# Attention fused with two feed-forward stages: the newer scores' maximum ahead of the older exponents' second half on VectorE, and a second buffer for three blocks' halves

## The chip, the cores and the metric

The kernel runs on one core of one Trainium2 chip. The metric is the device time of one execution in microseconds (us); lower is better. Three runs of the kernel before gave 980.55, 981.07 and 977.10 us, a median of 980.55 us. One more execution was recorded by the hardware profiler, and every row below comes from that one.

## What is computed

Batch 4, 8 heads of 64, 576 positions, model width 512. All inputs and outputs are float32.

```python
# 1. attention, causal by blocks of 64 positions
scores = (q @ k.T) / 8, where a block of keys later than the query's block is masked
attn   = exp(scores - rowmax); attn = attn / (rowsum + 1e-9)
x      = concat_heads(attn @ v)                     # (4, 576, 512)
# 2. feed-forward 1, with a layer norm (weights 512x2048 and 2048x512)
x = x + relu(layernorm(x) * g_ln @ w1) @ w2
# 3. Fourier mixing, then feed-forward 2
u = x + real(fft(fft(x, axis=positions), axis=width))
out = u + relu(layernorm(u) @ v1) @ v2
```

## The kernel before, in words

**Precision by halves.** A float32 operand is split into two float16 halves, a high and a low one, and a product is three TensorE passes (high·high, high·low, low·high). ScalarE writes the high half as a copy, and VectorE then writes the low half as operand minus high half. This pair stands everywhere: for the exponents it is `P` (lines 941 and 942 in `p_split`), for a block's normalized rows `xs` (lines 594 and 616), for the hidden layer `hT` (lines 658 and 659).

**Blocks.** The 576 positions of each batch row are cut into 128-row pieces. Blocks `("E", b)` hold rows 0 to 255, blocks `("F", b)` most of the others, and block `"L"` the rows left over. Attention for the E blocks runs first. Attention for the later rows runs in 16 units (batch row × pair of heads) of three slots each: j = 2 and j = 3 are 128 query rows against 384 and 512 keys for two heads, and j = 4 is 64 rows of two heads against 576 keys. While these 16 units run, TensorE also works on feed-forward 1 of the blocks that are ready (E2, E3, F0, F1 in that stretch), and the two sorts of matmul are interleaved in TensorE's order.

**One slot of the later rows** is made of six steps that a table of lags (`LG`) spreads over following slots: `a_s` (scores on TensorE into the PSUM tile `st`, two buffers), `a_exp` (VectorE takes the row maximum, line 1196, and scales it, line 1197; ScalarE takes the exponent into `e`, line 1200, once for each head), `a_norm_p` (ScalarE's high half of `P`, line 941; VectorE's low half, line 942; then a DMA that transposes `P` into `PT`, line 948), `a_pv` (TensorE multiplies `PT` by the values into `pv`, line 913; `pv` has two PSUM buffers), and `a_evac` (VectorE takes `rr`, a reciprocal of the sums, lines 955 and 958, and writes the rows `N`, line 1245; for j = 4 ScalarE writes them, line 1251). In slot t, `a_exp` is that of the scores of slot t-1, and `a_norm_p` that of slot t-2. `RK` is the rank of each of the six in one slot's emission: before, `a_norm_p` (0) comes first, then `a_pv` (1), `a_evac` (2), `a_s` (3) and `a_exp` (4).

**What sets the order.** The program is emitted step by step by `merge`, and a scheduler with priorities (`prio`) makes of it one instruction list for each engine. Each engine works through its list in that order. `tc.issue_after(x)` keeps an instruction behind x. All DMAs with `SPq` in the rows stand in one issuing list (SP's).

**Layer norm of a block** (`ln`, `ln_hi`, `ln_lo`): for each of a block's two 128-row halves t, VectorE normalizes into `xn` (line 585), ScalarE copies to `xs` (594), VectorE subtracts (616), and a DMA transposes `xs` into `xnT` (617). `xs` has one buffer, so the copy for t = 1 waits until the transposing DMA for t = 0 has read it.

**Feed-forward 1:** `gemm1` (line 649) fills one of the `g` PSUM buffers with 24 matmuls; the pair 658/659 empties it. `gemm2` is line 675.

Of the kernel before, what the change touches and what calls it, by code (L numbers as in the profile page):

```python
# [9 lines left out]
F16 = mybir.dt.float16  # L10
# [3 lines left out]
AF = mybir.ActivationFunctionType  # L14
ALU = mybir.AluOpType
# [3 lines left out]
DM = H * D  # L19
# [7 lines left out]
G2P = 1  # L27
ST = 2
RVE = 1
LATE = ((1, ("F", 0)), (1, ("F", 1)))  # L30
RAWE = 3
AP = 20
# [11 lines left out]
NB = 1  # L44
# [5 lines left out]
PSC = 2.0 ** 14  # L50
# [33 lines left out]
EB = 3  # L84
RV = 2
PTB = 3
RK = (3, 4, 0, 1, 2, 5, 5.5)
PLAIN2 = (("E", 0), ("F", 0))
YP = 60
S7P = 400  # L90
# [10 lines left out]
def fused_kernel(ctx: ExitStack, tc: tile.TileContext, io: dict):  # L101
    nc = tc.nc
# [4 lines left out]
    fpool = ctx.enter_context(tc.tile_pool(name="fpool", bufs=1))  # L107
# [422 lines left out]
    def ln(ffn, c):  # L530
        with ExitStack() as order:
            if (ffn, c) in LATE:
                order.enter_context(tc.issue_after(ff_last["g"]))
# [44 lines left out]
    def ln_hi(ffn, c, t):  # L578
        mv, y = lnst[ffn, c]
        own = (ffn, c) in TURN  # L580
        if own:
            xn = a_tile([128, DM], F32, "xn0", "xn0")
        else:
            xn = fpool.tile([128, DM], F32, tag="xn", bufs=1, name="xn")
        done = nc.vector.tensor_scalar(
            out=xn, in0=X[c][:, t, :], scalar1=mv[:, t, 0:1], scalar2=y[:, t:t + 1],
            op0=ALU.subtract, op1=ALU.mult,
        )
        if (ffn, c, t) == (1, ("E", 0), 1):
            ff_last["n"] = done.ins  # L590
        if own:
            return ln_turn(ffn, c, t, xn)
        xs = fpool.tile([128, 2, DM], F16, tag="xs", bufs=1, name="xs")
        nc.scalar.activation(out=xs[:, 0, :], in_=xn, func=AF.Copy)
        lnst[ffn, c, t] = (xn, xs)

    def ln_turn(ffn, c, t, xn):

        ps = g_tile([128, 4, 128], "xt")
        with ExitStack() as order:  # L600
            if "f" in ff_last:
                order.enter_context(tc.issue_after(ff_last["f"]))
            for k in range(KT):
                nc.tensor.transpose(
                    out=ps[:, k], in_=xn[:, 128 * k:128 * k + 128], identity=A["unit"]
                )
        to = xnT[ffn, c][:, :, :, t * 128:(t + 1) * 128]
        nc.scalar.activation(out=to[:, 0], in_=ps, func=AF.Copy)
        nc.vector.tensor_tensor(out=to[:, 1], in0=ps, in1=to[:, 0], op=ALU.subtract)
# [12 lines left out]
    def ln_steps(ffn, c):  # L622
        return [
            (0.0, lambda: ln(ffn, c)), (0.0, lambda: ln_hi(ffn, c, 0)),
            (0.0, lambda: (ln_lo(ffn, c, 0), ln_hi(ffn, c, 1))), (0.0, lambda: ln_lo(ffn, c, 1)),
        ]
# [201 lines left out]
    A = {}  # L828
# [10 lines left out]
    def a_open(bufs):  # L839
        ap_["ctx"] = ExitStack()  # L840
        ap_["p"] = ap_["ctx"].enter_context(tc.tile_pool(name="apool", bufs=1))
        ap_["b"] = bufs

    def a_tile(shape, dt, tag, name):
        return ap_["p"].tile(shape, dt, tag=tag, bufs=ap_["b"][tag], name=name)

    def a_close():
        ap_["ctx"].close()
# [90 lines left out]
    def p_split(e, P, n):  # L939

        nc.scalar.activation(out=P[:, 0, 0:n], in_=e, func=AF.Copy, scale=PSC)  # L941
        nc.vector.scalar_tensor_tensor(  # L942
            out=P[:, 1, 0:n], in0=e, scalar=PSC, in1=P[:, 0, 0:n], op0=ALU.mult, op1=ALU.subtract
        )

    def p_turn(P, blocks):
        PT = a_tile([128, blocks, 128], F16, "PT", "PT")
        nc.sync.dma_start_transpose(out=PT, in_=P.rearrange("p a k -> p (a k)"))
        return PT
# [180 lines left out]
    def a_zeros():  # L1130


        A["qz"] = [a_tile([128, 640], F32, "qz", f"qz{i}") for i in range(QZ)]
        for z in A["qz"]:
            for h in range(2):
                nc.gpsimd.memset(z[HALF[1 - h], 256 + 64 * h:320 + 64 * h], 0.0)
# [54 lines left out]
    def a_exp(u, j):  # L1191
        st = A.pop(("st", u, j))
        nh, w = st.shape[1:]
        q = sm.tile([128, 2, 2], F32, tag="aq", bufs=4, name="aq")
        mx, nb = q[:, 0, 0:nh], q[:, 1, 0:nh]
        nc.vector.tensor_reduce(out=mx, in_=st, axis=AX.X, op=ALU.max)
        nc.vector.tensor_scalar(out=nb, in0=mx, scalar1=-0.125, scalar2=None, op0=ALU.mult)  # L1197
        e = a_tile([128, nh, w], F32, "e", "e")
        for h in range(nh):
            nc.scalar.activation(  # L1200
                out=e[:, h], in_=st[:, h], func=AF.Exp, scale=0.125, bias=nb[:, h:h + 1],
            )
        A["e", u, j] = e.rearrange("p h k -> p (h k)")

    def a_norm_p(u, j):
        e = A.pop(("e", u, j))
        n = e.shape[-1]
        full = -(-n // 128) * 128
        P = a_tile([128, 2, full], F16, "P", "P")
        if full > n:  # L1210
            nc.gpsimd.memset(P[:, :, n:full], 0.0)
        p_split(e, P, n)
        A["PT", u, j] = p_turn(P, 2 * full // 128)

    @prio
# [58 lines left out]
    def attention_items(order):  # L1274
# [3 lines left out]
        def at(t, rank, fn, *a):  # L1278
            ev.setdefault(t, []).append((rank, len(ev.get(t, [])), fn, a))
# [9 lines left out]
        for t, (u, j) in enumerate(units):  # L1289
            at(t, RK[0], a_s, u, j)  # L1290
            at(t + lag[1], RK[1], a_exp, u, j)
            at(t + lag[2], RK[2], a_norm_p, u, j)
            at(t + lag[3], RK[3], a_pv, u, j)
            at(t + lag[4], RK[4], a_evac, u, j)
            if j == 4 and u[1] == NPAIR - 1:
                at(t + lag[5], RK[5], a_x, u[0])
                gives[t + lag[5]] = ("X1", ("F", u[0]))
# [283 lines left out]
    if True:  # L1581
# [15 lines left out]
        def a_switch():  # L1597
            a_close()
            ap_["first"] = False
            a_open(dict(  # L1600
                rawv=RV, qz=QZ, k=KB, vh=VB, vl=VB,
                e=EB, P=2, PT=PTB, N2=NB, N3=NB, N4=NB,
            ))
            a_zeros()

# [7 lines left out]
        ap_["first"] = True  # L1613
        a_open(dict(stage=ST, rv=RVE, rz=RAWE, warm=1, vh=2, vl=2, e=E1B[0], P=E1B[1], PT=E1B[2], xnT0=1, xn0=X0B, unit=1))
        warm = a_tile([128, 1], F32, "warm", "warm")
# [6 lines left out]
        w_signs(ap_["p"], WN[0], NZ[0])  # L1622
        AE = [e_items(b) for b in range(B)]
        A1 = [(0.0, a_switch, (("W", 1, 2, 3), ("X1", ("E", 3))), None)]
        A1 += attention_items([(b, p) for b in range(B) for p in range(NPAIR)])
        A1 += [(0.0, a_end, (), ("X1", "L"))]
# [204 lines left out]
```

## Time and profile before

| | |
|---|---|
| median of three runs | 980.55 us |
| the profiled execution's own time | 978.52 us |
| its span, first to last instruction | 976.7 us |
| TensorE (PE) matmul busy | 926.3 us, 95% |
| VectorE (DVE) busy | 689.4 us, 71% |
| ScalarE (ACT) busy | 490.6 us, 50% |
| GpSimd (POOL) busy | 73.0 us, 7% |

The span is 1.82 us shorter than the time of the same execution; the rest lies outside the first and last instruction. TensorE is the busiest engine over the whole span, but the share is a mean over stages. The later rows' attention, which the change touches, lies between about 150 and 420 us from the start; what follows until 460 us is its last blocks' layer norm and feed-forward 1. In rows of the timeline, the bracket at a row's end is the idle time of that engine just before the row, and the instruction that ended it.

### The profile page before, as it was taken

To read this page: it belongs to the slowest core of one execution; us is meant where nothing else is said; L and a number is where in the kernel's file an instruction comes from. 1 tells how busy PE (TensorE), PEld (TensorE's weight loads), DVE (VectorE), ACT (ScalarE), POOL (GpSimd) and SP (SyncE) were. 2 spreads that over 40 slices of the span, in tenths; PEclk is the share of its full clock that TensorE was granted. 3 is DMA by queue.
4 is the path that set the end of the run, shared out by engine and by line. 5 is a ranking of instruction groups with operands and counts; after the bars stand their busy time and mean duration, and the time that the engine had idled before them with its cause. 6 is when DMAs were issued, how large, how long until landed. Compare 5 with 4: busy or idle time off the path is not lost.

```text
span 976.7 us, 19426 instructions
## 1 busy us (share of the span) xinstructions
PE 926.3 (95%) x7694; PEld 687.5 (70%) x7694; DVE 689.4 (71%) x1770; ACT 490.6 (50%) x860; POOL 73.0 (7%) x183
## 2 busy tenths in 40 slices
PE   8887789999998999999899999999999999999998
PEld 5766634664664664767476777757688888888887
DVE  4887877565667567576489998589486676665754
ACT  5787844555555554437556663335144252352431
POOL 1000000002011020050011211100000000000000
PEclk9799989999999999999999999999999999999999
DMA  8658636669668666568407775101110210101100
GB/s 281 201 178 224 150 71 174 133 126 167 134 135 157 130 141 97 97 167 310 108 6 218 261 252 184 27 11 65 33 23 23 44 23 23 33 23 34 23 23 22
DMA packets 159179, 110.68 MB, mean 113 GB/s; under 512 B 134182, under 2 KB 141351, under 8 KB 157041
## 3 DMA queue, kind: packets, MB, share of 16 engines
q1 hardware_dynamic: 154640, 104.87, 41.5%
q0 software_dynamic: 2336, 4.06, 1.6%
q8 instruction: 60, 0.98, 0.4%
q10 hardware_dynamic: 2112, 0.52, 0.2%
q14 instruction: 31, 0.25, 0.1%
HBM read 63.93 MB, written 11.01 MB: 77 GB/s over the span
## 4 chain that ended last, share of the span: by engine, by line
PE 43%; DVE 8%; DMA 3%; ACT 3%; issue 1%; POOL 1%; SPq 0%; ACTq 0%; POOLq 0%; DVEq 0%
PE g L721 15%; PE s L771 13%; PE g L649 5%; PE g L702 4%; PE g L675 3%; DMA wr<-in_w 2%; DVE wq L346 1%; DVE ws L225 1%; DVE hT L659 1%; ACT junk L246 1%; PE pq L1522 1%; PE ya L1492 1%; DMA xnT2('F', 0)_8056<-xs 1%; ACT sign L224 1%; DVE x L1442 0%
## 5 line engine op out<-in xcount | busy, mean ns | idle before, releaser
L649 PEld LDWEIGHTS <-wq 128*128 128x128 f16 x2112 | 203.5, 98 | 41.7 <-issue 14.7
L675 PE MATMUL g<-wq,hT 128*128 128x512 f16 x768 | 185.8, 386 | 2.6 <-ACT hT L658 2.2
L721 PEld LDWEIGHTS <-wq 128*128 128x128 f16 x1344 | 131.5, 98 | 15.4
L675 PEld LDWEIGHTS <-hT 128*128 128x128 f16 x768 | 75.1, 99 | 91.6 <-issue 7.5
L771 PEld LDWEIGHTS <-hs 128*128 128x128 f16 x1176 | 115.1, 98 | 13.3
L913 PE MATMUL pv<-vh,PT 128*128 128x65 f16 (+1 forms) x704 | 101.5, 201 | 20.3 <-DMA PT<-P 11.3
L738 ACT ACTIVATE hr<-g,tk 128x256 f32<-128x256 f32 x112 | 47.0, 471 | 143.7 <-PE g L721 143.7
L913 PEld LDWEIGHTS <-PT 128*128 128x128 f16 x1056 | 80.5, 100 | 35.0 <-issue 17.4
L942 DVE SCALAR_TENSOR_TENSOR P<-e,P 128x768 f16<-128x768 f32 (+2 forms) x56 | 54.7, 976 | 68.9 <-ACT P L941 68.8
L746 DVE TENSOR_TENSOR hr<-hr 128x128 f32<-128x128 f32 x224 | 65.5, 293 | 48.2 <-ACT hr L738 40.3
L1200 ACT ACTIVATE e<-st,aq 128x384 f32<-128x384 f32 (+2 forms) x80 | 49.1, 652 | 94.1 <-DVE aq L1197 91.6
L771 PE MATMUL s<-tT,hs 128*128 128x256 f16 x672 | 75.6, 273 | 0.0
L659 DVE SCALAR_TENSOR_TENSOR hT<-g,hT 128x512 f16<-128x512 f32 x88 | 59.7, 681 | 16.1 <-ACT hT L658 15.8
L702 PE MATMUL g<-wq,hT 128*128 128x512 f16 x288 | 66.6, 391 | 0.0
L658 ACT ACTIVATE hT<-g 128x512 f16<-128x512 f32 x88 | 51.6, 587 | 28.9 <-PE g L649 28.7
L913 PE MATMUL pv<-vl,PT 128*128 128x64 f16 (+1 forms) x352 | 61.9, 201 | 0.0
L753 DVE TENSOR_TENSOR hs<-hr,hs 128x896 f16<-128x896 f32 x56 | 60.7, 1085 | 0.5
L771 PE MATMUL s<-tB,hs 128*128 128x256 f16 x504 | 57.3, 273 | 0.0
L224 ACT ACTIVATE sign<-wr 128x512 f16<-128x512 bf16 (+1 forms) x48 | 46.5, 969 | 16.4 <-DMA wr<-in_w 13.0
L752 ACT ACTIVATE hs<-hr 128x896 f16<-128x896 f32 x56 | 53.1, 948 | 1.6 <-DVE hr L746 1.6
L702 PEld LDWEIGHTS <-hT 128*128 128x128 f16 x288 | 28.6, 101 | 33.6 <-issue 3.1
L225 DVE SCALAR_TENSOR_TENSOR ws<-wr,sign 128x512 int32<-128x512 int32 (+1 forms) x48 | 41.2, 864 | 13.9 <-ACT sign L224 13.4
(414 smaller groups left out, 1511.9 us busy)
## 6 DMA issues: line engine op xcount, KB each, us to landing
wr<-in_w SPq DMA_DIRECT2D x16, 1023.5 KB, 6.0
wr<-in_w SPq DMA_DIRECT2D x32, 511.8 KB, 5.2
rawv<-in_vt SPq DMA_DIRECT2D x16, 320.0 KB, 3.0
k<-in_kt SPq DMA_DIRECT2D x16, 288.0 KB, 3.6
d<-ws SPq DMA_DIRECT2D x4, 1024.0 KB, 4.8
ws<-d SPq DMA_DIRECT2D x4, 1024.0 KB, 5.4
wt<-d SPq DMA_DIRECT2D x4, 1024.0 KB, 4.8
qz<-in_qt SPq DMA_DIRECT2D x32, 80.0 KB, 3.2
```

The lines of the kernel that those rows point to most:

```text
L224: nc.scalar.activation(out=z[:, :, :, 1], in_=r.bitcast(BF16)[:, :, :, 2], func=AF.Copy)
L649: nc.tensor.matmul(out=ps[:, i, :], lhsT=w1(ffn, k, wh, m), rhs=xt[:, xh, k, :], start=(n == 0), stop=(n == 3 * KT - 1),)
L659: done = nc.vector.scalar_tensor_tensor(out=h[:, :, 1, :], in0=ps, scalar=0.0, in1=h[:, :, 0, :], op0=ALU.max, op1=ALU.subtract,)
L675: nc.tensor.matmul(out=ps, lhsT=h[f // 4][:, f % 4, hh, t * 128:(t + 1) * 128], rhs=w2(ffn, f, wh), start=(f == 0 and hh == 0 and wh == 0) ...
L702: nc.tensor.matmul(out=g2["b"][t], lhsT=h[f // 4][:, f % 4, hh, t * 128:(t + 1) * 128], rhs=w2(ffn, f, wh), start=(f == 0 and hh == 0 and ...
L721: nc.tensor.matmul(out=ps[:, q, :], lhsT=w1(2, k, wh, i + 8 * q), rhs=xt[:, xh, k, :], start=(n == 0), stop=(n == 3 * KT - 1),)
L746: done = nc.vector.tensor_tensor(out=r[:, o], in0=r[:, a], in1=r[:, b], op=op)
L752: nc.scalar.activation(out=h[:, 0], in_=r[:, 1:8], func=AF.Copy)
L753: nc.vector.tensor_tensor(out=h[:, 1], in0=r[:, 1:8], in1=h[:, 0], op=ALU.subtract)
L771: nc.tensor.matmul(out=ps, lhsT=h[:, hh, hb], rhs=T[nm][:, wh, i], start=(i == 0 and hh == 0 and wh == 0), stop=(i == 7 and hh == 1),)
L913: nc.tensor.matmul(out=out[..., 0:w], lhsT=l, rhs=v[..., 0:w], start=(n == 0), stop=(n == len(mm) - 1))
L942: nc.vector.scalar_tensor_tensor(out=P[:, 1, 0:n], in0=e, scalar=PSC, in1=P[:, 0, 0:n], op0=ALU.mult, op1=ALU.subtract)
```

## The change

Three things are changed in the code. `a_exp` gets rank -1 and so comes first in a slot's emission. In `a_norm_p` the two instructions of `p_split` stand in the open, and the second one (VectorE's low half) is kept behind the newest scaled maximum, which `a_exp` leaves in `A["max"]`. And for the blocks E3, F0 and F1 of feed-forward 1 the second half's `xs` (t = 1) gets a buffer of its own, `xs1`.

```diff
+OWN = ((1, ("E", 3)), (1, ("F", 0)), (1, ("F", 1)))
...
-RK = (3, 4, 0, 1, 2, 5, 5.5)
+RK = (3, -1, 0, 1, 2, 5, 5.5)
...
-        xs = fpool.tile([128, 2, DM], F16, tag="xs", bufs=1, name="xs")
+        if (ffn, c) in OWN and t:
+            xs = a_tile([128, 2, DM], F16, "xs1", "xs1")
+        else:
+            xs = fpool.tile([128, 2, DM], F16, tag="xs", bufs=1, name="xs")
...
-        nc.vector.tensor_scalar(out=nb, in0=mx, scalar1=-0.125, scalar2=None, op0=ALU.mult)
+        got = nc.vector.tensor_scalar(
+            out=nb, in0=mx, scalar1=-0.125, scalar2=None, op0=ALU.mult
+        )
+        A["max"] = got.ins
...
-        p_split(e, P, n)
+        nc.scalar.activation(out=P[:, 0, 0:n], in_=e, func=AF.Copy, scale=PSC)
+        with tc.issue_after(A["max"]):
+            nc.vector.scalar_tensor_tensor(
+                out=P[:, 1, 0:n], in0=e, scalar=PSC, in1=P[:, 0, 0:n],
+                op0=ALU.mult, op1=ALU.subtract,
+            )
...
-                e=EB, P=2, PT=PTB, N2=NB, N3=NB, N4=NB,
+                e=EB, P=2, PT=PTB, N2=NB, N3=NB, N4=NB, xs1=1,
```

VectorE's list in a unit beside feed-forward 1's `gemm1` of block F0, before. `aq` is the maximum, `P` the low half of the exponents (1024, 576 and 768 wide for j = 3, 4 and 2), `hT` the emptying of a `g` buffer (the number tells which), `pw` the scale of a later unit's values:

```order
L942 SCALAR_TENSOR_TENSOR P<-e,P 128x1024
L659 SCALAR_TENSOR_TENSOR hT<-g_4236,hT 128x2x256
L955 TENSOR_SCALAR rr<-pv,pw 128x2
L1196 TENSOR_REDUCE aq<-st 128x1
L958 RECIPROCAL rr<-rr 128x2
L1197 TENSOR_SCALAR aq<-aq 128x1
L1245 TENSOR_TENSOR N_3851<-pv,rr 128x128
L955 TENSOR_SCALAR rr<-pv,pw 128x2
L942 SCALAR_TENSOR_TENSOR P<-e,P 128x576
...
L659 SCALAR_TENSOR_TENSOR hT<-g_4319,hT 128x2x256
L865 TENSOR_SCALAR pw<-pw 128x1
L1196 TENSOR_REDUCE aq<-st 128x2
```

The same stretch after:

```order
L1200 TENSOR_REDUCE aq<-st 128x1
L663 SCALAR_TENSOR_TENSOR hT<-g_4236,hT 128x2x256
L959 TENSOR_SCALAR rr<-pv,pw 128x2
L1201 TENSOR_SCALAR aq<-aq 128x1
L1221 SCALAR_TENSOR_TENSOR P<-e,P 128x1024
L962 RECIPROCAL rr<-rr 128x2
L1257 TENSOR_TENSOR N_3857<-pv,rr 128x128
L663 SCALAR_TENSOR_TENSOR hT<-g_4319,hT 128x2x256
L1200 TENSOR_REDUCE aq<-st 128x2
L959 TENSOR_SCALAR rr<-pv,pw 128x2
L1201 TENSOR_SCALAR aq<-aq 128x2
L1221 SCALAR_TENSOR_TENSOR P<-e,P 128x576
```

The maximum of j = 4 (`128x1`) has moved from behind the 1024-wide low half to ahead of it, and the maximum of the next unit's j = 2 from behind the 576-wide low half to ahead of it. `hT` of buffer 4319 has moved from behind the 576-wide low half to ahead of both that and the maximum. `N_3857` (the tile that was `N_3851`), which had no low half between it and the maximum of its slot, now has the 1024-wide one there.

VectorE's list in the layer norm of block F0, before (`xn` and `xs` as above; `N` is the rows of j = 2):

```order
L1161 SCALAR_TENSOR_TENSOR vl_3625<-rawv_3590,pw,vh_3624 128x10x64
...
L585 TENSOR_SCALAR xn<-XxF_2958,ln1('F', 0)_3924 128x512
L942 SCALAR_TENSOR_TENSOR P<-e,P 128x768
L616 TENSOR_TENSOR xs<-xn,xs 128x512
L585 TENSOR_SCALAR xn<-XxF_2958,ln1('F', 0)_3924 128x512
L1196 TENSOR_REDUCE aq<-st 128x2
L955 TENSOR_SCALAR rr<-pv,pw 128x2
L1197 TENSOR_SCALAR aq<-aq 128x2
L616 TENSOR_TENSOR xs<-xn,xs 128x512
L958 RECIPROCAL rr<-rr 128x2
L1245 TENSOR_TENSOR N_3773<-pv,rr 128x128
```

And after:

```order
L586 TENSOR_SCALAR xn<-XxF_2958,ln1('F', 0)_3924 128x512
L1165 SCALAR_TENSOR_TENSOR vl_3631<-rawv_3590,pw,vh_3630 128x10x64
L620 TENSOR_TENSOR xs<-xn,xs 128x512
L586 TENSOR_SCALAR xn<-XxF_2958,ln1('F', 0)_3924 128x512
L620 TENSOR_TENSOR xs_4025<-xn,xs_4025 128x512
L1200 TENSOR_REDUCE aq<-st 128x2
L959 TENSOR_SCALAR rr<-pv,pw 128x2
L1201 TENSOR_SCALAR aq<-aq 128x2
L1221 SCALAR_TENSOR_TENSOR P<-e,P 128x768
L962 RECIPROCAL rr<-rr 128x2
L1257 TENSOR_TENSOR N_3779<-pv,rr 128x128
```

The second `xs` now has a tile of its own (4025) and stands ahead of the maximum of j = 3; the 768-wide low half has moved from between the two `xn` to behind that maximum, just ahead of the reciprocal and `N`; and `vl`, the low half of a unit's values, which stood ahead of the first `xn`, stands behind it.

## Rows read from the trace of the kernel before

**Rows 1.** The page's head: the span.

```profile
span 976.7 us, 19426 instructions
```

**Rows 2.** Windows: busy of PE, PEld, DVE, ACT, POOL; TensorE clock; DMA share; GB/s.

```profile
150.00:460.00 310.00, 294.60 (x2557) 191.75 (x2556) 205.39 (x545) 163.67 (x285) 39.34 (x95) 0.99 0.68 149
```

**Rows 3.** Waits: who waited for whom; us in total, times, longest.

```profile
ACT e L1200 <- DVE aq L1197: 91.6, 45, 3.2
DVE P L942 <- ACT P L941: 68.8, 42, 2.3
```

**Rows 4.** Timeline of PE: start, us, what; in brackets idle before and releaser.

```profile
200.59 1.03 PE L649 MATMUL g<-xnT1('E', 2)_2013,wq 128*128 128x256 f16 x8 [2.06 <-DVE pw L865]
...
226.39 0.22 PE L913 MATMUL pv<-vh,PT 128*128 128x130 f16 x1 [2.22 <-DVE aq L1197]
...
271.76 1.58 PE L649 MATMUL g<-xnT1('E', 3)_2990,wq 128*128 128x256 f16 x13 [1.78 <-DVE hT L659]
...
309.56 0.27 PE L913 MATMUL pv<-vh,PT 128*128 128x130 f16 x1 [3.57 <-DVE N L1245]
...
349.02 1.03 PE L649 MATMUL g<-xnT1('F', 0)_3946,wq 128*128 128x256 f16 x8 [1.72 <-DVE pw L865]
...
378.72 0.19 PE L913 MATMUL pv<-vh,PT 128*128 128x65 f16 x1 [0.74 <-DVE N L1245]
```

**Rows 5.** Windows around two of these gaps; the last three columns are clock, DMA, GB/s.

```profile
224.00:228.00 4.00, 1.78 (x12) 0.90 (x12) 1.75 (x5) 2.14 (x4) 1.33 (x3) 0.94 0.58 116
228.00:232.00 4.00, 4.00 (x21) 2.07 (x20) 1.85 (x5) 2.24 (x3) 2.07 (x4) 0.63 1.04 231
308.00:312.00 4.00, 2.44 (x12) 1.45 (x13) 3.10 (x7) 2.50 (x4) 0.20 (x1) 0.68 0.67 117
312.00:316.00 4.00, 4.00 (x29) 2.01 (x28) 2.37 (x9) 2.71 (x6) 0.53 (x2) 0.89 0.98 212
```

**Rows 6.** Timeline of ACT and DVE in the layer norms of E3 and F0.

```profile
224.69 0.63 ACT L594 ACTIVATE xs<-xn 128x512 f16<-128x512 f32 x1 [3.16 <-DMA xnT1('E', 3)_2990<-xs]
...
301.72 0.55 DVE L585 TENSOR_SCALAR xn<-XxF,ln1('F', 0)_3924 128x512 f32<-128x512 f32 x1
...
307.66 0.63 ACT L594 ACTIVATE xs<-xn 128x512 f16<-128x512 f32 x1 [4.49 <-DMA xnT1('F', 0)_3946<-xs]
...
308.32 0.69 DVE L616 TENSOR_TENSOR xs<-xn,xs 128x512 f16<-128x512 f32 x1 [2.16 <-ACT xs L594]
...
309.12 0.29 DVE L1245 TENSOR_TENSOR N<-pv,rr 128x128 f32<-128x128 f32 x1
```

**Rows 7.** Timeline of ACT and DVE around the gap that ends at 349.02.

```profile
345.15 0.74 ACT L1200 ACTIVATE e<-st,aq 128x576 f32<-128x576 f32 x1 [2.44 <-DVE aq L1197]
...
346.64 0.76 DVE L942 SCALAR_TENSOR_TENSOR P<-e,P 128x576 f16<-128x576 f32 x1 [1.25 <-ACT P L941]
...
347.24 0.58 ACT L658 ACTIVATE hT<-g 128x512 f16<-128x512 f32 x1
...
348.28 0.68 DVE L659 SCALAR_TENSOR_TENSOR hT<-g,hT 128x512 f16<-128x512 f32 x1
...
349.98 0.88 DVE L1161 SCALAR_TENSOR_TENSOR vl<-rawv,pw,vh 128x640 f16<-128x640 f32 x1
```

**Rows 8.** Groups by line: shapes, count | busy us, mean ns | idle before, releasers.

```profile
L942 DVE SCALAR_TENSOR_TENSOR P<-e,P 128x768 f16<-128x768 f32 (+2 forms) x56 | 54.7, 976 | 68.9 <-ACT P L941 68.8
...
L1196 DVE TENSOR_REDUCE aq<-st 128x2 f32<-128x768 f32 (+2 forms) x48 | 46.6, 970 | 0.0
```

**Rows 9.** Timeline of SP, POOL and PEld from 240 to 245 us.

```profile
240.43 1.44 SPq L948 DMA_TRANSPOSE PT<-P  x1
...
242.12 0.78 PEld L913 LDWEIGHTS <-PT 128*128 128x128 f16 x18
...
244.28 0.20 POOL L1211 MEMSET P<- 128x128 f16 x1 [9.46 <-DMA PT<-P]
```

**Rows 10.** Timeline of PE behind the stage.

```profile
479.03 11.22 PE L675 MATMUL g<-wq,hT 128*128 128x512 f16 x42 [2.21 <-ACT hT L658]
```

## The prediction

> **What bounds the kernel now.** I read the views in this order: the windows, to see which stage has idle time on the busiest engine; TensorE's timeline in that stage, for the gaps and what ended them; the waits of VectorE and ScalarE; and the timelines of both just ahead of each gap.
>
> The profiled execution took 978.52 us, of which 976.7 is the span [rows 1]. The change touches the attention of the later rows, in the window from 150 to 460 us. There TensorE is busy for 294.60 of 310 us while VectorE is busy for 205.39 and ScalarE for 163.67 [rows 2]. So the stage runs at TensorE's pace with 310 - 294.6 = 15.4 us of gaps, and these are what an order of VectorE's list can win. Five gaps hold 2.06 + 2.22 + 1.78 + 3.57 + 1.72 = 11.35 us of it; each was ended by VectorE [rows 4]. The other 4.05 us lie in short gaps, like the one of 0.74 [rows 4].
>
> The five are of two sorts. At 226.39 and 309.56 a `pv` product waits for a PSUM buffer that the rows `N` empty. In both, ScalarE had been standing before the layer norm's second `xs`, 3.16 and 4.49 us, because the DMA that reads the first one had not landed; behind it VectorE stood 2.16 us at the low half of `xs`, with `N` behind that in its list [rows 6]. These two gaps also cost clock. In the 8 us around the first the granted clock was 0.94 and 0.63, around the second 0.68 and 0.89 [rows 5]: each time 4 x (0.06 + 0.37) or 4 x (0.32 + 0.11) = 1.72 us of full-speed work, part of it spent at the lower level, 1.2 GHz. At 200.59, 271.76 and 349.02 `gemm1` waits for a `g` buffer, that is for `hT`. In the last of them ScalarE's exponent had waited 2.44 us for VectorE's maximum, ScalarE's half of `hT` came only at 347.24 and VectorE's at 348.28, behind the low half of `P`, for which VectorE had itself waited 1.25 us [rows 7]. It is a ping-pong: over the run ScalarE's exponents wait 91.6 us for maxima, VectorE's low halves 68.8 us (42 times, 1.6 each) for ScalarE's high halves [rows 3]. Neither engine is full; each stands idle for the other.
>
> **The change part by part.** No arithmetic is added. VectorE issues as many maxima and low halves as before, of mean 0.97 and 0.98 us [rows 8]; only their places move.
>
> *Second buffer, block E3.* Its second `xs` can now be made together with the first, long before 224 us, so the 3.16 us wait goes. The gap of 2.22 us goes with it, and the 1.72 us of clock: 3.94 us.
>
> *Second buffer, block F0.* ScalarE's 4.49 us wait goes, but the new order puts other work ahead of `N`. From the start of the first `xn` the list now holds `xn` 0.55, `vl` 0.88, `xs` 0.69, `xn` 0.55, ScalarE's copy 0.63, `xs` 0.69, a maximum 0.97, the low half 0.98 and `N` 0.29 [rows 6 to 8]: 6.2 us, with three small ones about 6.7 (an estimate: 0.5 for the three). Before, it was 309.12 + 0.29 - 301.72 = 7.7. So `N` gains 1.0 us by its own list, and up to 1.6 more where the first `xn` itself starts earlier by one removed wait for a high half [rows 3]. Of the 3.57 us then 1.0 to 2.6 are left; I take 1.3, a saving of 2.3, since one slot's wait is likely gone. With so short a gap I take the 1.72 us of clock as saved too: 4.0 us. F1 has no gap of this sort among the five; its buffer counts as nothing.
>
> *Maximum first, beside `gemm1`.* Where the gap ended at 349.02, the maximum of j = 4 no longer stands behind a low half, so the exponent's 2.44 us go, and `hT` of the waiting buffer now precedes the next maximum and low half. `hT` comes at least 2.44 us earlier against a gap of 1.72 [rows 4, 7]. The gaps at 200.59 and 271.76 wait for the same thing. All three: 5.56 us. Next to be late there is `hT` behind `vl` in the same unit, whose place does not change.
>
> *The short gaps.* Of 4.05 us I take 1.0 as gone; zero and 4.05 are the ends.
>
> *TensorE's own list.* 48 more `pv` matmuls than before follow another `pv` matmul instead of a longer one. Eighteen in a row had their weights loaded in 0.78 us, 0.043 each [rows 9], so at most 48 x 0.043 = 2.1 us and at least nothing. Beside a longer matmul they were not free either; I take 0.7.
>
> *What is added as waits.* The low half of a slot now waits for the next slot's scores and maximum, and behind it in VectorE's list stand `rr`, `N` and `hT`. With slots of about 270 us / 48 = 5.6 us the scores are there a slot ahead in the units I followed, so the low half is not later than before by more than the maximum it lets pass. The transposing DMA behind it took 244.28 - 240.43 = 3.85 us until `P` was free again [rows 9], and its product comes two slots later, so it is covered. In SP's list the two query loads of most units now stand ahead of j = 3's transposing DMA. Their issue is not among my rows; the nearest is the 1.44 us of a transposing one, so 0 to 2.9 us late, under the same two slots. A wait of one more `N` here and there is likely; I take 2.0 us for new gaps in all, between 0 and the 15.7 us worked out under the third rival.
>
> *Sum.* 3.94 + 4.0 + 5.56 + 1.0 - 0.7 - 2.0 = 11.8 us, so 978.52 - 11.8 = 966.7 us against the profiled execution. Its 978.52 lies 2.03 below the median of the runs (980.55). I add half of that and predict 968 us. If every gap and both clock losses went, 15.4 + 3.4 = 18.8 us, it would be 960 us.
>
> **Rivals.**
>
> *Only the buffer pays.* The gaps before `gemm1` and before `pv` would then come from there being two `g` and two `pv` buffers, and an order of VectorE would move them, not remove them. For it: all five gaps wait for a PSUM buffer [rows 4]. Against it: the buffers' readers are late because VectorE and ScalarE stand idle, not because they are busy [rows 2, 3]. Gain 3.94 + 4.0 - 0.7 = 7.2, so 972 us. The Trainium skill, "Perfetto Trace Analysis", section Optimization Strategy, says that bubbles which repeat on the engine that ought to be full can mean too few PSUM or SBUF buffers. By that rule the three gaps of about 1.9 us, one in each stretch of `gemm1`, stay, and this rival is the outcome.
>
> *Given back later.* At 479.03 TensorE waits 2.21 us for ScalarE's `hT` [rows 10], in a stretch where ScalarE and VectorE prepare the second feed-forward's weights. If that preparation sets the pace and does not start earlier, TensorE only waits longer there: no change, 978 to 980 us. Against it: the preparation is started by the end of the attention, which moves with TensorE.
>
> *Slower: `N` behind the low half.* In every slot the low half, 0.98 us, now stands between the maximum and `N`. Each `N` frees one of two `pv` buffers, and the gap of 0.74 us ended by `N` [rows 4] shows that there is little spare time. If VectorE does not get its removed waits (1.6 us each) back ahead of `N`, each of the 16 units loses one 0.98: 15.7 us, of which the buffer's 7.2 are taken off, so 8.5 us slower, 988 us. It decides if `N` leaves later than before by more than the spare time once in a unit. The Trainium skill, "TensorE: Matmul & The Clock Gate", section on the architecture of the array, calls the lists of ScalarE and VectorE strict FIFO. The trace agrees, the `N` of 309.12 stood behind an `xs` it does not need [rows 6]; so one late high half would hold back everything.
>
> **How the numbers follow.** My forecast has a chance of 0.55 (962 to 971 us), only the buffer 0.18 (972), given back 0.17 (979), slower 0.10 (988). Half a percent of the median is 4.9 us, about what a measurement of this kernel can tell: faster means under 975.6, slower over 985.5. Faster: all of the forecast, 0.16 of the second and 0.04 of the third, 0.75. Slower: 0.08 of the last. The same: the other 0.17. The range is 960, where all gaps are gone, to 980, where nothing is gained; it leaves out little but the slower case.
>
> **What would show it.** Right: in the profile after, ScalarE's waits for maxima and VectorE's for high halves fall well under half of 91.6 and 68.8 us; TensorE's gaps between 150 and 460 us shrink from 15.4 to about 6; there is no wait of ScalarE at the second `xs` of E3 and F0, and the granted clock stays at 1.00 around E3's. Wrong: waits at `gemm1` for `hT` as long as before (then the buffer counts decide), new gaps before `pv` ended by `N` once in a unit (the slower case), or a longer gap than 2.21 us near 470 us (given back).

## The result, and where the profile after shows the time

The change took 966.3 us (median of four runs, 962.85 to 968.14) against 980.81 us of the kernel before (four runs, 977.1 to 983.43): a ratio of 0.9849, interval 0.9823 to 0.9875. Measured once more, among the experiments, it was 968.44 us and 0.9857 (0.9834 to 0.988). The profiled execution of the kernel after took 966.11 us, of which 964.3 is the span, 12.4 us less than [rows 1]. The forecast was 968 us.

In the kernel after, `gemm1` is line 653, `hT` 662 and 663, `pv` 917, the maximum 1200 and 1201, the exponent 1207, the halves of `P` 1219 and 1221, `xs` 598 and 620, `N` 1257 and 1263. First the page's head, and the window of the later rows' attention, with the columns of [rows 2]:

```profile
span 964.3 us, 19399 instructions
```

```profile
150.00:460.00 310.00, 305.46 (x2658) 200.84 (x2657) 215.87 (x574) 175.63 (x310) 42.14 (x96) 1.00 0.67 155
```

TensorE's gaps in it fell from 15.4 to 4.5 us, and the granted clock is at 1.00. The waits, as in [rows 3]:

```profile
ACT e L1207 <- DVE aq L1201: 64.1, 40, 5.0
...
DVE hT L663 <- ACT hT L662: 37.0, 36, 2.4
...
DVE vl L1165 <- ACT vh L1164: 16.8, 13, 1.8
...
ACT P L1219 <- DMA PT<-P: 15.5, 10, 3.0
```

VectorE's wait for the high half of `P`, 68.8 us before, is down to 1.8 us; ScalarE's wait for the maximum, 91.6 us before, fell by 30% only. Three waits are longer: VectorE's for `hT` (15.8 us before) and for `vh`, the high half of a unit's values (2.7 us before), and ScalarE's for the transposing DMA that frees a buffer of `P` (1.3 us before), because the low half, and with it that DMA, now comes later. TensorE's timeline, as in [rows 4] and [rows 10]:

```profile
301.29 0.22 PE L917 MATMUL pv<-vh,PT 128*128 128x130 f16 x1 [2.27 <-DVE N L1257]
...
367.31 0.19 PE L917 MATMUL pv<-vh,PT 128*128 128x65 f16 x1 [0.98 <-DVE N L1257]
...
410.98 9.22 PE L679 MATMUL g<-wq,hT 128*128 128x512 f16 x42 [0.36 <-DVE hT L663]
...
465.19 12.12 PE L679 MATMUL g<-wq,hT 128*128 128x512 f16 x54 [2.25 <-ACT hT L662]
...
545.39 0.39 PE L1534 MATMUL pq<-c_so,y 128*128 128x128 f16 x2 [2.07 <-ACT y L1511]
```

Of the five gaps of [rows 4] one is left, F0's, and that shortened; beside `gemm1` none is left. The row at 465.19 answers to [rows 10], and it comes 13.84 us earlier.

To size each term I take the start of one and the same matmul in both traces: the one that masks the scores of a unit's first slot (`MATMUL st<-never,late`). That of the fourth unit, before, after, and in the trace of the second measurement, whose profiled execution took 974.84 us:

```profile
195.61 0.20 PE L935 MATMUL st<-never,late 64*128 64x64 bf16 x2
```

```profile
197.71 0.20 PE L939 MATMUL st<-never,late 64*128 64x64 bf16 x2
```

```profile
200.97 0.20 PE L939 MATMUL st<-never,late 64*128 64x64 bf16 x2
```

| stretch, by the clock of before (us) | what lay there before | took before | took after | saved | took, second trace |
|---|---|---|---|---|---|
| 0 to 195.61 | ahead of the first gap | 195.61 | 197.71 | -2.10 | 200.97 |
| 195.61 to 213.65 | gap at 200.59 | 18.04 | 15.82 | 2.22 | 15.82 |
| 213.65 to 233.43 | gap at 226.39 (E3) and its clock | 19.78 | 15.73 | 4.05 | 15.73 |
| 262.68 to 280.45 | gap at 271.76 | 17.77 | 15.82 | 1.95 | 15.82 |
| 294.41 to 315.44 | gap at 309.56 (F0) and its clock | 21.03 | 18.14 | 2.89 | 19.86 |
| 344.38 to 362.08 | gap at 349.02 | 17.70 | 15.82 | 1.88 | 15.82 |
| 395.01 to 479.03, the row of [rows 10] | short gaps | 84.02 | 82.44 | 1.58 | 82.29 |
| the other four in between | short gaps | 105.08 | 103.71 | 1.37 | 106.24 |
| 479.03 to the end | | 497.67 | 499.11 | -1.44 | 500.55 |

The sum saved is 12.4 us. The stage itself, from the second row to the next to last, took 283.42 us before and 267.48 after and so saved 15.94 us; the rest was lost ahead of it and behind it. In the second trace the stage took 271.58 us and saved 11.84. What was saved at E3 and beside `gemm1` is the same there to 0.01 us. The 4.10 us between the two executions lie at F0 (1.72 us: about the same gap, but with a loss of clock behind it) and around F1 (2.52 us). In the second trace:

```profile
304.61 0.22 PE L917 MATMUL pv<-vh,PT 128*128 128x130 f16 x1 [2.34 <-DVE N L1257]
...
374.46 0.19 PE L917 MATMUL pv<-vh,PT 128*128 128x65 f16 x1 [2.26 <-DVE N L1257]
...
472.55 1.80 PE L679 MATMUL g<-wq,hT 128*128 128x512 f16 x4 [2.24 <-ACT hT L662]
```

F1's gap, the second row, was 0.98 us in the first trace.

### The profile page after: what moved, and what is told of

Read it like the earlier page. It is cut to its first block, busy times and chain, and to the rows that moved or that the text cites. A ratio compares the mean times of both kernels' runs of the same rounds, so it can differ in the third digit from the quotient of the medians.

```text
span 964.3 us, 19399 instructions
## 1 busy us (share of the span) xinstructions
PE 924.6 (96%) x7694; PEld 689.5 (72%) x7694; DVE 688.7 (71%) x1770; ACT 491.8 (51%) x860; POOL 74.8 (8%) x183
## 4 chain that ended last, share of the span: by engine, by line
PE 46%; DVE 7%; DMA 4%; ACT 3%; issue 1%; POOL 0%; SPq 0%; ACTq 0%; POOLq 0%
PE g L725 15%; PE s L775 13%; PE g L653 7%; PE g L679 4%; PE g L706 4%; DMA wr<-in_w 2%; DVE wq L347 1%; ACT junk L247 1%; DVE ws L226 1%; PE pq L1534 1%; DMA xnT2('F', 0)_8056<-xs 1%; ACT sign L225 1%; PE ya L1504 1%; DVE hT L663 1%; PE pv L917 1%
## 5 line engine op out<-in xcount | busy, mean ns | idle before, releaser
L679 PE MATMUL g<-wq,hT 128*128 128x512 f16 x768 | 180.5, 379 | 3.0 <-ACT hT L662 2.2
L725 PEld LDWEIGHTS <-wq 128*128 128x128 f16 x1344 | 131.5, 98 | 15.4
L917 PE MATMUL pv<-vh,PT 128*128 128x65 f16 (+1 forms) x704 | 98.4, 201 | 15.7 <-DMA PT<-P 10.7
L917 PEld LDWEIGHTS <-PT 128*128 128x128 f16 x1056 | 76.4, 99 | 34.0 <-DMA PT<-P 15.9
L1207 ACT ACTIVATE e<-st,aq 128x384 f32<-128x384 f32 (+2 forms) x80 | 48.9, 652 | 64.8 <-DVE aq L1201 64.1
L706 PE MATMUL g<-wq,hT 128*128 128x512 f16 x288 | 66.0, 388 | 0.0
L917 PE MATMUL pv<-vl,PT 128*128 128x64 f16 (+1 forms) x352 | 58.7, 200 | 0.0
L1200 DVE TENSOR_REDUCE aq<-st 128x2 f32<-128x768 f32 (+2 forms) x48 | 46.7, 973 | 12.5 <-PE st L939 9.4
L1219 ACT ACTIVATE P<-e 128x768 f16<-128x768 f32 (+2 forms) x48 | 41.2, 858 | 17.4 <-DMA PT<-P 15.5
```

The costliest lines, as they stand in the source:

```text
L679: nc.tensor.matmul(out=ps, lhsT=h[f // 4][:, f % 4, hh, t * 128:(t + 1) * 128], rhs=w2(ffn, f, wh), start=(f == 0 and hh == 0 and wh == 0) ...
L706: nc.tensor.matmul(out=g2["b"][t], lhsT=h[f // 4][:, f % 4, hh, t * 128:(t + 1) * 128], rhs=w2(ffn, f, wh), start=(f == 0 and hh == 0 and ...
L725: nc.tensor.matmul(out=ps[:, q, :], lhsT=w1(2, k, wh, i + 8 * q), rhs=xt[:, xh, k, :], start=(n == 0), stop=(n == 3 * KT - 1),)
L917: nc.tensor.matmul(out=out[..., 0:w], lhsT=l, rhs=v[..., 0:w], start=(n == 0), stop=(n == len(mm) - 1))
```

## The experiments

My theory after the result: the new order ends the gaps beside `gemm1`, the buffer those in the layer norms, and the two add up. The rivals: one part does it all, or the gaps beside `gemm1` end because of another place of `hT`, not because the ping-pong of ScalarE and VectorE ends. Each ratio below is to the kernel before on the same chip (medians 980.85 to 982.14 us); it is not quite the quotient of the two medians, from which it differs by up to 0.2%.

**The buffer alone.**

```diff
-RK = (3, -1, 0, 1, 2, 5, 5.5)
+RK = (3, 4, 0, 1, 2, 5, 5.5)
...
-        with tc.issue_after(A["max"]):
...
```

> Only the second xs buffer for E3, F0, F1; ranks and low half's place as before. Theory A (two parts that add: the buffer ends the gaps in the layer norms, the order those before gemm1): gap of 2.22 us at E3 gone with its clock loss, gap of 3.57 us at F0 down to 1 to 2 us, the three gemm1 gaps of about 1.9 us each still there; 6 to 9 us faster than before, ratio 0.991 to 0.994. Rival B (the order alone does it): ratio 0.999 to 1.001. Rival C (only the buffer pays, the order only moves gaps): ratio as the full change, 0.983 to 0.988.

Measured: 977.2 us, ratio 0.9951 (0.9933 to 0.997), less than theory A expected. **The order alone:**

```diff
-OWN = ((1, ("E", 3)), (1, ("F", 0)), (1, ("F", 1)))
+OWN = ()
```

> Ranks and the low half behind the newer maximum as in the change, xs with one buffer for all blocks. Theory A: the three gemm1 gaps gone (5.6 us) and most short gaps, the gaps at E3 and F0 still there at 2 to 4 us each with clock loss; 5 to 8 us faster, ratio 0.992 to 0.995. Rival B: ratio as the full change, 0.983 to 0.988. Rival C: ratio 0.999 to 1.001, gemm1 gaps of about 1.9 us still there.

Measured: 972.15 us, ratio 0.9913 (0.9886 to 0.994), more than theory A expected. The product of the two, 0.9864, is near the change's 0.9849: as far as the intervals tell, the parts add on time. Neither does it all. TensorE's timeline with the buffer alone, and then with the order alone:

```profile
201.50 1.03 PE L653 MATMUL g<-xnT1('E', 2)_2013,wq 128*128 128x256 f16 x8 [1.74 <-DVE pw L869]
...
225.36 0.22 PE L917 MATMUL pv<-vh,PT 128*128 128x130 f16 x1 [0.27 <-DVE N L1256]
...
306.67 0.22 PE L917 MATMUL pv<-vh,PT 128*128 128x130 f16 x1 [2.16 <-DVE N L1256]
```

```profile
234.78 0.20 PE L917 MATMUL pv<-vh,PT 128*128 128x65 f16 x1 [1.06 <-DMA PT<-P]
...
302.42 0.22 PE L917 MATMUL pv<-vh,PT 128*128 128x130 f16 x1 [3.50 <-DVE N L1257]
...
370.89 0.19 PE L917 MATMUL pv<-vh,PT 128*128 128x65 f16 x1 [1.75 <-DVE N L1257]
```

The gaps beside `gemm1` stay with the buffer alone and are gone with the order alone, which settles who ends them. The gap at E3 has two remedies: the buffer takes it to 0.27 us, and the order removes it without the buffer. F0's gap, 3.50 us with the order alone, needs the buffer to come down to the change's 2.27.

**The new rank of the maximum, without the low half held behind it.**

```diff
-        with tc.issue_after(A["max"]):
-            nc.vector.scalar_tensor_tensor(
+        nc.vector.scalar_tensor_tensor(
...
```

> The full change, but the low half isn't kept behind the newer maximum: the scheduler puts the low half ahead of the maximum again, while ScalarE's and TensorE's lists are nearly those of the change and hT of the waiting buffer stands right behind the 576-wide low half instead of behind rr, a reciprocal and three scale steps. If the removed ping-pong of maximum and high half is what ends the gemm1 gaps: ScalarE's waits for maxima back to 85 to 95 us, gemm1 gaps of 1 to 2 us back, 4 to 6 us slower than the change, ratio to before 0.989 to 0.992. If the place of hT in the lists does it: no gemm1 gap, ratio 0.983 to 0.988.

Measured: 970.76 us, ratio 0.9891 (0.9872 to 0.9911). Its waits:

```profile
ACT e L1207 <- DVE aq L1201: 91.6, 44, 3.1
...
DVE P L1220 <- ACT P L1219: 54.4, 37, 2.6
```

TensorE's timeline, two rows of five:

```profile
199.83 1.47 PE L653 MATMUL g<-xnT1('E', 2)_2013,wq 128*128 128x256 f16 x12 [0.80 <-DVE hT L663]
...
339.80 1.47 PE L653 MATMUL g<-xnT1('F', 0)_3946,wq 128*128 128x256 f16 x12 [1.11 <-DVE hT L663]
```

The ping-pong is back, 91.6 and 54.4 us, and so are gaps beside `gemm1`: 0.80 and 0.37 us at E2, 0.62 at E3, 1.11 and 0.37 at F0, 3.27 in all against 5.56 before and none with the hold. So in this one trace about two fifths of their end are the rank's, three fifths the hold's.

**The low half held, but the halves of `P` behind `N` in each slot**, so that `hT` stands again where it stood among ScalarE's copies and behind VectorE's small steps on `pw`.

```diff
-RK = (3, -1, 0, 1, 2, 5, 5.5)
+RK = (3, -1, 2.5, 1, 2, 5, 5.5)
```

> The full change, but the step of the low half comes after the pv evacuation in a slot's emission: maxima stand ahead of the older low halves as in the change for j = 3 and 4, while hT of the waiting buffer stands where it stood before in VectorE's and ScalarE's lists (behind the 576-wide low half, the reciprocal and the scale steps). If the removed ping-pong alone ends the gemm1 gaps: no gap over 0.5 us there, ratio 0.984 to 0.988. If the place of hT does it: gaps of 1 to 2 us there, ratio 0.989 to 0.993.

Measured: 975.18 us, ratio 0.993 (0.9904 to 0.9955); the profiled execution took 979.77 us. The time is what I expected if `hT`'s place mattered, but the trace says otherwise:

```profile
234.00 0.20 PE L917 MATMUL pv<-vh,PT 128*128 128x65 f16 x1 [2.12 <-DMA PT<-P]
...
244.69 0.23 PE L917 MATMUL pv<-vh,PT 128*128 128x130 f16 x1 [1.85 <-DMA PT<-P]
...
345.93 1.03 PE L653 MATMUL g<-xnT1('F', 0)_3946,wq 128*128 128x256 f16 x8 [0.45 <-DVE pw L869]
...
378.00 0.19 PE L917 MATMUL pv<-vh,PT 128*128 128x65 f16 x1 [2.66 <-DVE rr L959]
```

Beside `gemm1` 0.45 us is left of 5.56, and the ping-pong is gone: VectorE waits 3.9 us for high halves of `P`. So `hT`'s old place behind those steps did not make the gaps. But the expectation is wrong in one point: on VectorE `hT` does not stand behind the 576-wide low half here, but ahead of it, as in the change:

```profile
345.19 0.68 DVE L663 SCALAR_TENSOR_TENSOR hT<-g,hT 128x512 f16<-128x512 f32 x1
...
347.76 0.75 DVE L1221 SCALAR_TENSOR_TENSOR P<-e,P 128x576 f16<-128x576 f32 x1
```

So whether the earlier maximum ends the gaps, or the low half's leaving its place ahead of `hT`, isn't separated by these runs; the hold does both.

Two gaps in this trace, 2.12 and 1.85 us, are ended by `P`'s transposing DMA, which the later low half starts later. The row at 378.00 is F1's gap, which the change has too. How much of the time each costs is not shown; gaps of 1.06 to 1.43 us ended by that DMA stand near 236 us in three other kernels, one of them (the buffer alone, 1.43) with the low half in its old place.

**The buffer for F0 and F1 only**, twice, and **for E3 only**.

```diff
-OWN = ((1, ("E", 3)), (1, ("F", 0)), (1, ("F", 1)))
+OWN = ((1, ("F", 0)), (1, ("F", 1)))
```

> The change with the second buffer for F0 and F1 only; E3's second xs waits for the first one's transposing DMA again. Theory A (the gap at E3 had two sufficient remedies: with the new order alone there was no gap of TensorE at E3 although ScalarE still waited 1.6 us there, so the buffer of E3 adds nothing to the order): 0.983 to 0.987 of the kernel before, no gap ended by VectorE near 226 us, granted clock 1.00 there. Theory B (the terms add as in my prediction, E3's buffer is worth 3.94 us): 0.987 to 0.991, and a gap of about 2 us near 226.

> The second buffer for F0 and F1 only, a second time, since its first time (0.9911) and its trace (no gap at E3, gain of 4.05 us there as in the change) disagree. If E3's buffer is worth nothing under the new order: 0.984 to 0.988, and the first time was one of several levels that the clock behind the gaps of about 2 us makes. If it is worth something: 0.989 to 0.993 again.

> The change with the second buffer for E3 alone. Theory A (of the buffers only F0's and F1's shorten a gap under the new order): the time of the order alone, 0.989 to 0.993, and a gap of about 3.5 us at F0. Theory B (E3's buffer is worth something that the gaps don't show, since without it the kernel was 0.5% slower than with it): 0.985 to 0.989.

Measured: 0.9911 (0.9889 to 0.9933) and 0.9908 (0.9876 to 0.9939) for F0 and F1; 0.9897 (0.9872 to 0.9923) for E3. In both traces of the first there is no gap ended by VectorE near 226 us and the clock there is 1.00, as theory A said, and yet the time is theory B's, 0.5% over the change's on the same chip. By the ratios, one buffer without the other gains next to nothing on the order alone (0.9913), both together 0.6%. The traces don't show why: the stage of the table took 270.94 and 269.18 us with the buffer for F0 and F1, 272.52 with that for E3, 272.24 with none, but 267.48 and 271.58 in two executions of the change itself. It stays open.

**A third buffer for `P`**, with every engine's order as in the change.

```diff
-                e=EB, P=2, PT=PTB, N2=NB, N3=NB, N4=NB, xs1=1,
+                e=EB, P=3, PT=PTB, N2=NB, N3=NB, N4=NB, xs1=1,
```

> The change with three buffers for P in place of two; the order on every engine is that of the change. In the trace of the change ScalarE's high half waited 15.5 us, ten times, for the DMA that frees P, a wait that before had been 1.3 us. Theory A (that wait costs TensorE nothing: behind it VectorE's maximum waits for the newest scores anyway, and the gap at F0 is set by the maximum, the low half and N behind those scores): the wait goes, the gap of about 2.3 us at F0 stays at 1.8 to 2.4, and the time is that of the change within 0.25%. Theory B (the new wait is what my term of 2.0 us for new waits is made of, and its 1.1 us at F0 makes half of that gap): the gap at F0 falls to about 1.2 us and the time is 0.1 to 0.4% under the change's.

> The change itself once more, to stand beside the three others on one chip: 0.982 to 0.988 of the kernel before. In its own profile the gap at F0 is 1.8 to 2.6 us and that at F1 about 1 us; the time of the landmark ahead of the stage (the first scores of the later rows, 134.0 to 137.4 us in six traces so far, with one and the same order of TensorE up to there) differs by a microsecond or two from execution to execution whatever the kernel.

Measured on the same chip: 967.8 us, 0.9852 (0.9829 to 0.9876), beside the change's 968.44 and 0.9857. TensorE's timeline with the third buffer:

```profile
236.06 0.20 PE L917 MATMUL pv<-vh,PT 128*128 128x65 f16 x1 [1.09 <-DMA PT<-P]
...
301.35 0.22 PE L917 MATMUL pv<-vh,PT 128*128 128x130 f16 x1 [1.14 <-DVE N L1257]
```

ScalarE's wait for that DMA is gone, and F0's gap halved, as theory B said: the wait did stand in F0's chain. F1's gap is gone too, and there the size of the wait differs by execution. ScalarE's high half of `P` ahead of F1's gap, in the first trace of the change and then in the second:

```profile
356.03 0.84 ACT L1219 ACTIVATE P<-e 128x768 f16<-128x768 f32 x1 [1.61 <-DMA PT<-P]
```

```profile
363.19 0.84 ACT L1219 ACTIVATE P<-e 128x768 f16<-128x768 f32 x1 [3.78 <-DMA PT<-P]
```

F1's gap was 0.98 us behind the wait of 1.61, and 2.26 us behind that of 3.78; with the buffer for F0 and F1 only it was 1.74 us behind 2.38. All this is too small to show in the time by itself.

**The low half behind `N` in two slots only**, those of the gaps left at F0 and F1.

```diff
+HOLD = (((2, 1), 2), ((3, 1), 3))
...
+        last = A["nrow"] if (u, j) in HOLD else A["max"]
+        with tc.issue_after(A["max"]), tc.issue_after(last):
...
+                at(t + lag[2], 2.5, prio(a_low), u, j)
```

> The change, but in two slots, those whose N ended the gaps of 2.27 us (F0) and 0.98 us (F1) in the trace of the change, the low half of P is kept behind N. Theory A (N stands behind the low half there and the low half can wait a slot): the gap at F0 falls by the low half's 0.95 us to about 1.3, that at F1 by 1.2 us to nothing, and the time is 1 to 3 us under the change's, 0.10 to 0.35%. Theory B (as where the low half stood behind the rows N in every slot: the transposing DMA then lands late): new gaps of 1 to 2 us ended by that DMA, one or two slots behind, and the time is the change's or up to 0.3% over it.

Measured: 970.21 us, 0.9891 (0.9871 to 0.9911), by the two ratios 0.3% over the change on the same chip (0.2% by the medians; the intervals overlap). TensorE's timeline:

```profile
299.60 0.22 PE L918 MATMUL pv<-vh,PT 128*128 128x130 f16 x1 [2.36 <-DVE N L1265]
...
307.94 0.20 PE L918 MATMUL pv<-vh,PT 128*128 128x65 f16 x1 [2.68 <-DMA PT<-P]
```

Theory B: the held low half's DMA is late a slot on, 2.68 us. F0's own gap did not shrink either: ScalarE's high half ahead of it waited 2.00 us for a buffer of `P`, where it had waited 1.11 in the trace of the change, and that took back the 0.95 us. At F1 the gap fell to 0.34 us, and 1.17 us ended by that DMA stand a slot on.

**F0's second `xn` and `xs` a slot later, behind `N`**, with two buffers for `P`, and then with three.

```diff
+    def ln_late():
+        with tc.issue_after(A["nrow"]):
+            ln_hi(1, ("F", 0), 1)
+            ln_lo(1, ("F", 0), 1)
...
```

> The change, and in F0's layer norm the second half's normalizing and its low half of xs (0.55 and 0.69 us, and the 0.7 us that VectorE waits between them for ScalarE's copy) are issued a slot later, behind the rows N that end the gap there, in place of ahead of them. Theory A (that gap is the sum of what stands ahead of N in VectorE's list): N comes 1.2 to 1.9 us earlier against the maximum ahead of it, the gap of 2.3 us at F0 falls to 0.2 to 1.1, the clock after it stays at 1.00, feed-forward 1 of F0 some 16 us later starts without a gap, and the time is 1 to 4 us under the change's: 0.981 to 0.985 of the kernel before. Theory B (N there waits for the scores, not for the list): gap and time as in the change, 0.985.

> The same with three buffers for P, which took the gap at F0 from 2.3 to 1.1 us by itself. Theory A: no gap over 0.5 us at F0, the stage's gaps fall to 2 to 3 us, and the time is 0.980 to 0.984 of the kernel before. Theory B (what the stage gains beyond the change is given back behind 465 us, where VectorE is busy for 38 of 40 us: the trace with the third P buffer was 15.4 us ahead at 464 us and 10.0 ahead at the end): 0.985 with the stage ahead by 15 us or more at about 465 us.

Measured: 966.99 us, 0.9849 (0.982 to 0.9878) with two; 963.53 us, 0.9814 (0.9788 to 0.984) with three. With two, F0's gap is gone, as theory A said, but the time is that of the change. F1's gap, behind a wait of 2.38 us for a buffer of `P`, lies between the change's 0.98 and 2.26 us:

```profile
364.25 0.19 PE L934 MATMUL pv<-vh,PT 128*128 128x65 f16 x1 [1.73 <-DVE N L1274]
```

With three, neither is left, and the window of the stage is the fullest of all:

```profile
150.00:460.00 310.00, 307.36 (x2667) 201.62 (x2666) 217.56 (x577) 176.04 (x310) 42.81 (x100) 1.00 0.71 157
```

The stage of the table took 265.30 us. But 5.62 us were given back behind it, in a profiled execution of 969.23 us: the three gaps behind 460 us were 2.20, 2.07 and 2.38 us, and by windows of 4 us all three cost clock, 5.08 us of full-speed work, where before one did, 1.72. By its median this version is 18 us under the kernel before. It is 3 to 5 us under the change, but those two intervals overlap.

## Why the prediction was right, and where its terms were not

The time was right to 1.7 us, and the mechanism was the forecast one. But that the sum of 11.8 us came so near the span's 12.4 us is partly luck: errors of opposite sign met, and the second trace of the change has a span 8.8 us longer than the first.

- *Second buffer, block E3* (3.94): the stretch saved 4.05 us, and with the buffer alone the gap fell to 0.27. The attribution was too narrow: the order alone closes it as well.
- *Second buffer, block F0* (4.0, with 1.3 us of gap left): 2.27 us are left and 2.89 were saved. The list ahead of `N` was the right one, but the estimate left out a wait that ScalarE hands on to VectorE. From the start of the first `xn` to the end of `N` it took 300.85 + 0.29 - 292.54 = 8.60 us, where the prediction had about 6.7 and before it was 7.7. `N` came earlier all the same, because the first `xn` started earlier: 5.22 us behind the mask matmul of its unit (287.32 us), where it had been 7.31 (294.41 us). Of these 2.09 us the prediction had allowed up to 1.6. The timeline of ScalarE ahead of that gap, and then VectorE's:

```profile
293.49 0.84 ACT L1219 ACTIVATE P<-e 128x768 f16<-128x768 f32 x1 [1.11 <-DMA PT<-P]
294.24 0.81 ACT L1164 ACTIVATE vh<-rawv,pw 128x640 f16<-128x640 f32 x1
...
297.19 0.63 ACT L598 ACTIVATE xs<-xn 128x512 f16<-128x512 f32 x1 [1.62 <-DVE xn L586]
```

```profile
292.54 0.71 DVE L586 TENSOR_SCALAR xn<-XxF,ln1('F', 0)_3924 128x512 f32<-128x512 f32 x1
295.09 0.89 DVE L1165 SCALAR_TENSOR_TENSOR vl<-rawv,pw,vh 128x640 f16<-128x640 f32 x1 [1.83 <-ACT vh L1164]
...
298.46 1.22 DVE L1200 TENSOR_REDUCE aq<-st 128x2 f32<-128x1024 f32 x1
...
300.85 0.29 DVE L1257 TENSOR_TENSOR N<-pv,rr 128x128 f32<-128x128 f32 x1
```

  ScalarE's high half of `P` waits 1.11 us for a buffer, so `vh` is late, and VectorE stands 1.83 us at `vl`, with `xs`, the maximum and `N` behind it. The prediction had `vl`'s 0.88 us but no wait at it. The wait of [rows 6] for the first `xs`' DMA is gone, as said: what is left, 1.62 us, is for `xn`.
- *Maximum first, beside `gemm1`* (5.56): 2.22 + 1.95 + 1.88 = 6.05 us, and no gap left. The rank without the hold leaves 3.27 us; the hold without the rank was not run. The rule of the Trainium skill that the second rival cited ("Perfetto Trace Analysis", section Optimization Strategy: repeating bubbles can mean too few buffers) names a possible cause, and it is not that of these three: the order alone ended them with the buffers as they were. It does fit what is left at F0 and F1, which a third buffer of `P` halved and ended.
- *Short gaps, bunched matmuls, new waits* (1.0 - 0.7 - 2.0 = -1.7): the terms that were sized worst. They came to 1.58 + 1.37 = +2.95 us, and in the second trace to 0.57; the difference lies around F1. The bunching costs nothing that shows: the two units from 315.44 to 344.38, with no gap in either trace, took 28.94 us before and 28.99 after. Of the new waits, ScalarE's for a buffer of `P` costs TensorE its part of F0's gap and the whole of F1's.
- *Given back later*: 1.44 us, not all; 2.88 in the second trace, and up to 5.62 in those of the experiments. [rows 10] came back as 2.25 us, so the sign "longer than 2.21 us" was there by a hair. Behind it the gap at 545.39 grew to 2.07 us (1.05 in the trace of before, at 560.02), and one at 623.86 to 1.79 (1.07, at 636.26). VectorE is busy for 38.16 of the 40 us from 520 to 560, before for 38.49; that it sets the pace there was not tried.
- *Ahead of the stage*: -2.10 us, of which 1.75 stand before the later rows' first such matmul, at 153.13 us before and 154.88 after. TensorE's list is one and the same up to there in all kernels run, and over fourteen traces that matmul starts between 152.16 and 157.84 us: it differs from execution to execution. (The landmark at 134.0 to 137.4 us in the expectation above is the last masking matmul of the E blocks, 18 us earlier.)
- *What would show it*: gaps of about 6 us came out as 4.5, and 6.7 in the second trace; the clock around E3 was 1.00 in both. ScalarE's waits for maxima "well under half" failed, 64.1 of 91.6 us. They did not need to fall that far: TensorE's gaps beside `gemm1` are gone all the same.
- *Slower: `N` behind the low half*: it shows at F0 and F1 (2.27 and 0.98 us; 2.34 and 2.26 in the second trace), not once in a unit. With the low half behind `N` everywhere the kernel was slower than the change, 0.993 against 0.985. The rule of the Trainium skill that stood beside this rival, strict FIFO lists ("TensorE: Matmul & The Clock Gate", section on the architecture of the array) agrees with the last experiment: two VectorE instructions moved behind `N` took F0's gap from 2.27 us to nothing.

## What to carry to other kernels

Where two engines take turns on halves of a precision pair and each idles for the other, put the newer operand's reduction ahead of the older half and hold the older one behind it; but follow that half's DMA, for a half that is held too long makes its reader late. Ahead of a late instruction, count the waits of the engine that feeds its list, not only the durations in the list. A gap may have several remedies, so try them alone and together. Whether small fixes that show nothing one by one show together is suggested here by the last experiment, but not clear of the noise. And take two traces of one kernel before you size a gap from one.

## What the runs showed of the hardware that I had not expected

A gap of about 2.3 us costs clock in one execution and none in the next. In the first execution of the change F0's gap of 2.27 us was followed by a clock of 1.00; in the second the gap was 2.34 us and the clock fell to 0.68 and 0.89, that is 4 x (0.32 + 0.11) = 1.72 us of full-speed work, as in [rows 5]. The windows around the gap, in the first and then in the second:

```profile
298.00:302.00 4.00, 1.73 (x27) 1.23 (x26) 3.96 (x9) 1.94 (x3) 0.00 (x0) 1.00 0.72 140
302.00:306.00 4.00, 4.00 (x32) 2.08 (x30) 2.48 (x7) 1.90 (x4) 0.27 (x2) 1.00 0.95 211
```

```profile
304.00:308.00 4.00, 3.39 (x17) 1.85 (x18) 3.46 (x10) 2.49 (x4) 0.08 (x1) 0.68 0.83 151
308.00:312.00 4.00, 4.00 (x28) 1.95 (x27) 1.31 (x4) 1.49 (x4) 0.43 (x3) 0.89 0.89 214
```

In four other traces with a gap there, 2.31 us cost 1.68 us by such windows (the buffer for F0 and F1 only), 2.70 us cost nothing (the same kernel again), 3.50 us cost 1.72 (the order alone) and 3.13 us cost 3.44 (the buffer for E3 only). What decides it is not shown.

One kernel's runs spread: with the buffer for F0 and F1 only, they lay between 968.66 us at a mean clock of 0.988 and 976.39 at 0.982. Nor does a single trace size every gap: in the two of the change F0's was 2.27 and 2.34 us, but F1's 0.98 and 2.26, because the wait for the DMA that frees `P` was 1.61 us in the one and 3.78 in the other.
